# Windowed attention and a routed two-layer FFN: wider score slots, scatters without order among themselves, and q, k, v loaded in other pieces

## The chip, the cores and the metric

The kernel runs on one core of one Trainium2 chip. The metric is the device time of one execution in microseconds (us). A core has a matrix engine (PE, whose weight loads are listed apart as PEld), a vector engine (DVE), an activation engine (ACT), a general engine (POOL) and a sync engine (SP) that only issues transfers; 16 DMA engines move data between HBM and the on-chip memory. PE writes to PSUM, the accumulators; everything else lies in SBUF.

## The reference

```python
def _attn_ref(q, k, v):                       # (8, 8, 576, 64) each: batch, head, position, width
    scores = np.matmul(q, k.transpose(0, 1, 3, 2)) / np.sqrt(64)
    scores = np.where(np.abs(pos[:, None] - pos[None, :]) <= 32, scores, -1e9)
    return softmax(scores) @ v

def _moe_ref(x, modality_id, w_gate, modality_bias, w1, w2):   # x: (4608, 512), 8 experts
    logits = x @ w_gate + modality_bias[modality_id]
    e_idx = np.argmax(logits, axis=1)                          # one expert for a token
    gate_w = softmax(logits)[np.arange(N), e_idx]
    for e in range(8):                                         # w1[e]: 512x1024, w2[e]: 1024x512
        out[e_idx == e] = gate_w * (np.maximum(x @ w1[e], 0) @ w2[e])
```

## The kernel before

The work has two stages. The attention stage loops over 8 batches. The FFN stage loops over tiles of 256 tokens that have the same expert. They meet in a scratch array `scr` in HBM, where each expert has a region of rows.

Loads of a batch. q and k come in two groups of four heads, 96 partitions with six consecutive positions each (L227, runs of 1.5 KB). q is cast to bf16 on POOL (L233), k on ACT (L235). v comes in five blocks of 128 positions (L241, runs of 256 B) and is cast on POOL (L242). All of these loads are issued on SP's queue, as are the token ids (L155) and the zeros that are written to the first 256 rows of each expert's region (L199).

A batch has four pairs of heads. For each, PE transposes q and k in six pieces of 96 positions (L254); DVE copies q's transposes out of PSUM (L259), ACT copies k's (L261); one PSUM buffer `tp` serves both and the routing. Scores are computed transposed, key blocks j against the 192 queries that each can see (96 for the last block, L272). They lie side by side in slots of 192, blocks 0, 1 and 4 in one PSUM tile, 2 and 3 in another. ACT takes the exponent of each tile (L275, 960 and 768 columns), DVE multiplies by the mask (L277). The output block m then takes two products with `pt` as the weights: the 128 first columns of slot m (L288), and for m > 0 the 64 last columns of slot m - 1 (L295):

```python
nc.tensor.matmul(o_t[:, m - m0, h, :], pt[:, h, c0:c0 + P], vt[:, m, 2 * hp + h, :], ...)
if m > 0:
    nc.tensor.matmul(o_t[0:64, m - m0, h, :], pt[:, h, c1:c1 + 64], vt[:, m - 1, 2 * hp + h, :], ...)
```

DVE divides by the sum of the row, which an added column of ones in v delivers (L300, L301).

Routing of a batch. For each of five blocks PE transposes the attention output (L311), DVE copies it (L313), and PE multiplies by the gate (L315). Some 17 small DVE instructions find the expert, the gate weight and the token's row in the expert's region (`di`, L361). Five indirect DMAs issued by POOL scatter the rows of 1,088 bytes (output, gate weight, token number) into `scr` (L364). After batch 0 the weights of two experts are loaded from POOL's queue (L178, L181). After batch 7 DVE builds a table of tiles (L390 to L453).

FFN, tile i: SP loads 256 rows of `scr` (L463), PE transposes them (L467), multiplies by w1 (L490), ACT applies the relu (L492), PE multiplies by w2 (L504), DVE scales by the gate weight (L507), and POOL scatters 128 rows twice to the output by an indirect DMA (L509), with indices that DVE makes (L499). 19 tiles always run; six more stand behind a condition.

The order of instructions on each engine and all waits are made by the framework: it schedules at build time, earlier program text first, and derives a wait from each pair of accesses to the same memory. Two scatters into `scr`, or two into the output, count as such a pair, because their rows are known only at run time. Engines execute their own instructions in order.

Of the kernel before, what the change touches and what calls it, by code (L numbers as in the profile page):

```python
# [21 lines left out]
FP32 = mybir.dt.float32  # L22
# [9 lines left out]
def kernel(  # L32
# [14 lines left out]
    P = 128  # L47
# [7 lines left out]
    R = 6  # L55
    SP_ = S // R
# [21 lines left out]
    PW = 896  # L78
    SLOT = {0: 0, 1: 192, 4: 384, 2: 512, 3: 704}
    mask = const.tile([P, PW], BF16)  # L80
    nc.gpsimd.memset(mask[:], 1.0)
    for j in (0, 1, 2, 3):
        m_ap = mask[:, SLOT[j]:SLOT[j] + 192]
        nc.gpsimd.affine_select(out=m_ap, in_=m_ap, compare_op=ALU.is_ge, fill=0.0,
                                base=0, pattern=[[1, 192]], channel_multiplier=-1)
        nc.gpsimd.affine_select(out=m_ap, in_=m_ap, compare_op=ALU.is_ge, fill=0.0,
                                base=64, pattern=[[-1, 192]], channel_multiplier=1)
    m_ap = mask[:, SLOT[4]:SLOT[4] + 96]
# [25 lines left out]
    ids_i, ids_f = iota_f([P, B, NM], [[S, B], [P, NM]], -32, 1)  # L114
# [29 lines left out]
    nc.sync.dma_start(mb_bc[:], moe_modality_bias.partition_broadcast(P))  # L144

    mid = const.tile([P, B, NM], FP32)
    mid64 = const.tile([P, B, NM], mybir.dt.int64)
    nc.gpsimd.memset(mid64[:].bitcast(I32), 0)
    idv = moe_modality_id.rearrange("(b s) -> s b", s=S)
    with nc.allow_non_contiguous_dma(reason="token ids, once"):  # L150
        for m in range(NM):
            p0 = 32 if m == 0 else 0
            p1 = 96 if m == NM - 1 else P
            s0 = P * m - 32
            nc.sync.dma_start(mid64[p0:p1, :, m:m + 1], idv[s0 + p0:s0 + p1, :].unsqueeze(2))  # L155
    nc.vector.tensor_copy(mid[:].rearrange("p b m -> p (b m)").unsqueeze(2),
                          mid64[:].rearrange("p b m -> p (b m)").bitcast(I32)
                          .rearrange("p (n two) -> p n two", two=2)[:, :, 0:1])
    bias = const.tile([P, B * NM, E], FP32)
    msel = const.tile([P, B * NM], FP32)  # L160
    mtmp = const.tile([P, B * NM, E], FP32)
    for m_ in range(n_mod):
        nc.vector.tensor_scalar(out=msel[:], in0=mid[:].rearrange("p b m -> p (b m)"),
                                scalar1=float(m_), scalar2=None, op0=ALU.is_equal)
        dst = bias if m_ == 0 else mtmp
        nc.vector.tensor_tensor(
            out=dst[:], in0=msel[:].unsqueeze(2).to_broadcast([P, B * NM, E]),
            in1=mb_bc[:, m_, :].unsqueeze(1).to_broadcast([P, B * NM, E]), op=ALU.mult)
        if m_:
            nc.vector.tensor_tensor(out=bias[:], in0=bias[:], in1=mtmp[:], op=ALU.add)  # L170
# [18 lines left out]
    qT_t = [const.tile([P, 32 + S], BF16, name=f"qT{i}") for i in range(2)]  # L189
# [3 lines left out]
    for t_ in x_t:  # L193
        nc.gpsimd.memset(t_[:, :, HD // 2 + 2:ROW // 2], 0)

    zero = const.tile([P, TT // P, ROW // 2], I32)
    nc.gpsimd.memset(zero[:], 0)
    for e in range(E):
        nc.sync.dma_start(scr[N * e:N * e + TT, :].rearrange("(s p) c -> p s c", p=P), zero[:])  # L199
    for t_ in qT_t:  # L200
        nc.gpsimd.memset(t_[:, 0:32], 0.0)
    for t_ in p_t:
        nc.gpsimd.memset(t_[:, :, SLOT[4] + 96:SLOT[4] + 128], 1.0)
    for t_ in v_t:
        nc.gpsimd.memset(t_[:, :, :, D:D + 1], 1.0)
# [5 lines left out]
    with (  # L211
        tc.tile_pool(name="ld", bufs=3) as ld,
        tc.tile_pool(name="ldb", bufs=4) as ldb,
        tc.tile_pool(name="kt", bufs=2) as ktp,
# [3 lines left out]
        tc.tile_pool(name="ps_t", bufs=1, space=bass.MemoryType.PSUM) as ps_t,  # L218
        tc.tile_pool(name="ps_m", bufs=1, space=bass.MemoryType.PSUM) as ps_m,
    ):  # L220
        for b in range(B):

            qb, kb = [None, None], [None, None]
            for g in range(2):
                for nm, src, dst in (("q", q, qb), ("k", k, kb)):
                    f_ = ld.tile([SP_, 4, R * D], FP32, tag="qkf")
                    nc.sync.dma_start(  # L227
                        f_[:], src[b, 4 * g:4 * g + 4].rearrange("h (p r) d -> p h (r d)", r=R))
                    c_ = ldb.tile([SP_, R, 4 * D], BF16, tag=nm + "b")
                    o_ap = c_[:].rearrange("p r (h d) -> p h r d", h=4)  # L230
                    i_ap = f_[:].rearrange("p h (r d) -> p h r d", r=R)
                    if nm == "q":
# [3 lines left out]
                    dst[g] = c_  # L236
            vt = v_t[b % 2]
            for j in range(NM):
                s0 = min(P * j, S - P)
                f_ = ld.tile([P, H, D], FP32, tag="vf")  # L240
                nc.sync.dma_start(f_[:], v[b, :, s0:s0 + P, :].rearrange("h s d -> s h d"))  # L241
                nc.gpsimd.tensor_copy(vt[:, j, :, 0:D], f_[:])  # L242
# [3 lines left out]
            for hp in range(H // 2):  # L246
                g, l = hp // 2, 2 * (hp % 2)
                it = b * 4 + hp
                qT = qT_t[it % 2]
                kT = ktp.tile([P, S], BF16, tag="kT")  # L250
                for src, dst, eng in ((qb[g], qT[:, 32:32 + S], "v"), (kb[g], kT[:], "a")):
                    tp = ps_t.tile([P, S], BF16, tag="tp")
                    for i in range(R):
                        nc.tensor.transpose(tp[:, SP_ * i:SP_ * (i + 1)],  # L254
                                            src[:, i, D * l:D * l + P], ident[0:SP_, 0:SP_])
                    o_ap = dst.rearrange("d (p r) -> d p r", r=R)
                    i_ap = tp[:].rearrange("d (r p) -> d p r", p=SP_)
                    if eng == "v":
                        nc.vector.tensor_copy(o_ap, i_ap)  # L259
                    else:  # L260
                        nc.scalar.copy(o_ap, i_ap)  # L261
# [3 lines left out]
                for js, s_t, o0, wd in (((0, 1, 4), sA, 0, 480), ((2, 3), sB, 512, 384)):  # L265
                    for j in js:
                        c0 = SLOT[j] - o0
                        k0 = P * j if j < 4 else S - P
                        q0 = P * j
                        w_ = 192 if j < 4 else 96  # L270
# [4 lines left out]
                    nc.scalar.activation(pt[:, :, o0:o0 + wd], s_t[:, :, 0:wd], ACT.Exp, scale=scale)  # L275
                    w2_ = 512 if o0 == 0 else 384
                    nc.vector.tensor_tensor(  # L277
                        out=pt[:, :, o0:o0 + w2_], in0=pt[:, :, o0:o0 + w2_],
                        in1=mask[:, o0:o0 + w2_].unsqueeze(1).to_broadcast([P, 2, w2_]), op=ALU.mult)
# [3 lines left out]
                for o_t, m0, ms in ((oA, 0, (0, 1, 2)), (oB, 3, (3, 4))):  # L283
                    first = True
                    for m in ms:
                        for h in range(2):
                            c0 = SLOT[m]
                            nc.tensor.matmul(  # L288
                                o_t[:, m - m0, h, :], pt[:, h, c0:c0 + P], vt[:, m, 2 * hp + h, :],
                                start=first, stop=(m == 0),  # L290
                                skip_group_check=True)
                            first = False
# [14 lines left out]
            lg = ps_m.tile([P, NM, E], FP32, tag="m")  # L307
# [10 lines left out]
            nc.vector.tensor_tensor(out=lo[:], in0=lg[:], in1=bias[:, NM * b:NM * b + NM, :], op=ALU.add)  # L318
# [24 lines left out]
            rk = ps_m.tile([P, NM + 1, E], FP32, tag="m")  # L343
# [112 lines left out]
    def ffn(tiles, pools):  # L456
# [38 lines left out]
        def down(i):  # L495
# [33 lines left out]
    with (  # L529
# [45 lines left out]
```

## Time and profile before

| | |
|---|---|
| time, median of 3 runs | 503.09 us (500.39 to 504.54) |
| the profiled execution | 506.83 us |
| its span, first to last instruction | 505.1 us |
| PE busy | 344.3 us (68%) |
| DVE, ACT, POOL busy | 200.5, 144.2, 140.9 us |
| attention stage, to the last `di` | 0 to 308.7 us |
| FFN stage, to the last scatter's issue | 322.5 to 493.8 us |

Times of day below are us from the span's start. A busy share is an average over both stages, which have different limits.

### The profile page before, as it was taken

To read this page: it belongs to the slowest core of one execution; us is meant where nothing else is said; L and a number is where in the kernel's file an instruction comes from. 1 tells how busy PE (TensorE), PEld (TensorE's weight loads), DVE (VectorE), ACT (ScalarE), POOL (GpSimd) and SP (SyncE) were. 2 spreads that over 40 slices of the span, in tenths; PEclk is the share of its full clock that TensorE was granted. 3 is DMA by queue.
4 is the path that set the end of the run, shared out by engine and by line. 5 is a ranking of instruction groups with operands and counts; after the bars stand their busy time and mean duration, and the time that the engine had idled before them with its cause. 6 is when DMAs were issued, how large, how long until landed. Compare 5 with 4: busy or idle time off the path is not lost. (4 is left out here: it accounts for less than half of the span.)

```text
span 505.1 us, 7239 instructions
## 1 busy us (share of the span) xinstructions
PE 344.3 (68%) x2694; PEld 228.9 (45%) x2712; DVE 200.5 (40%) x529; ACT 144.2 (29%) x197; POOL 140.9 (28%) x225
## 2 busy tenths in 40 slices
PE   0477642675687587686785871299999987878900
PEld 0244431453454354454554540176766655546500
DVE  2434723654555654654645547122232131311400
ACT  2333432154135242341432310033323322313200
POOL 9122326334063332332300302102321222212320
PEclk9999999999999999999999999999999999999965
DMA  9999699955936785621000100302323223232120
GB/s 181 238 236 205 128 218 250 207 129 141 228 87 151 167 189 135 117 54 42 32 21 0 51 0 21 119 1 88 108 86 108 84 75 99 84 108 86 64 84 21
DMA packets 75238, 56.09 MB, mean 111 GB/s; under 512 B 49472, under 2 KB 70720, under 8 KB 75200
## 3 DMA queue, kind: packets, MB, share of 16 engines
q1 hardware_dynamic: 66576, 36.93, 33.6%
q0 software_dynamic: 8624, 18.66, 12.9%
q8 instruction: 23, 0.38, 0.3%
q14 instruction: 15, 0.12, 0.1%
HBM read 122.79 MB, written 17.76 MB: 278 GB/s over the span
## 5 line engine op out<-in xcount | busy, mean ns | idle before, releaser
L364 POOL DMA_INDIRECT scr<-xt,di x40 | 41.3, 1033 | 150.4 <-DMA scr<-xt,di 69.0
L492 ACT ACTIVATE hT<-ph 128x512 bf16<-128x512 f32 x76 | 45.4, 597 | 122.3 <-PE ph L490 122.3
L490 PE MATMUL ph<-xT,w 128*128 128x256 bf16 x608 | 70.6, 275 | 0.0
L509 POOL DMA_INDIRECT out_dram<-ys,ix x38 | 36.9, 970 | 115.6 <-DMA out_dram<-ys,ix 56.6
L504 PE MATMUL py<-w,hT 128*128 128x512 bf16 x286 | 67.6, 379 | 0.9
L490 PEld LDWEIGHTS <-w 128*128 128x128 bf16 x608 | 59.4, 99 | 7.2
L275 ACT ACTIVATE pt<-sA 128x960 bf16<-128x960 f32 x32 | 31.0, 970 | 75.0 <-PE sA L272 68.8
L288 PEld LDWEIGHTS <-pt 128*128 128x128 bf16 x320 | 29.3, 108 | 40.9 <-DVE pt L277 23.0
L295 PEld LDWEIGHTS <-pt 128*64 128x64 bf16 x256 | 32.7, 128 | 30.6 <-issue 12.9
L277 DVE TENSOR_TENSOR pt<-pt,mask 128x1024 bf16<-128x1024 bf16 x64 | 44.4, 723 | 3.9 <-ACT pt L275 3.9
L288 PE MATMUL oA<-vt,pt 128*128 128x65 bf16 x192 | 33.8, 239 | 17.2 <-DVE pt L277 15.4
L499 DVE TENSOR_TENSOR ix<-xg,pen_i 128x2 int32<-128x2 int32 x19 | 3.1, 161 | 105.7 <-DMA out_dram<-ys,ix 93.5
L504 PEld LDWEIGHTS <-hT 128*128 128x128 bf16 x304 | 29.8, 98 | 32.0
L288 PE MATMUL oB<-vt,pt 128*128 128x65 bf16 x128 | 30.1, 235 | 13.4 <-POOL vt L242 12.6
L507 DVE TENSOR_SCALAR ys<-py,xg 128x512 f32<-128x512 f32 x38 | 27.5, 748 | 17.0 <-PE py L504 15.4
L295 PE MATMUL oB<-vt,pt 128*64 128x65 bf16 x128 | 33.7, 263 | 0.0
L295 PE MATMUL oA<-vt,pt 128*64 128x65 bf16 x128 | 33.7, 263 | 0.0
L467 PE MATMUL tp<-ident,xg 128*128 128x128 bf16 x152 | 12.5, 229 | 29.1 <-DMA xg<-scr 29.1
L259 DVE COPY qT<-tp 128x576 bf16<-128x576 bf16 x32 | 24.2, 757 | 18.8 <-PE tp L254 17.5
L313 DVE COPY xT<-tp 128x512 bf16<-128x512 bf16 x40 | 16.9, 423 | 25.9 <-PE tp L311 25.9
L261 ACT COPY kT<-tp 128x576 bf16<-128x576 bf16 x32 | 20.4, 638 | 22.1 <-PE tp L254 21.8
L315 PE MATMUL lg<-wg_sb,xT 128*128 128x8 bf16 x160 | 10.7, 173 | 23.4 <-DVE xT L313 23.4
(254 smaller groups left out, 417.1 us busy)
## 6 DMA issues: line engine op xcount, KB each, us to landing
w<-in_moe_w_dram POOLq DMA_DIRECT2D x42, 1024.0 KB, 8.0
xg<-scr SPq DMA_DIRECT2D x19, 272.0 KB, 3.2
scr<-zero SPq DMA_DIRECT2D x8, 272.0 KB, 3.4
scr<-xt,di POOLq DMA_INDIRECT x40, 2.5
out_dram<-ys,ix POOLq DMA_INDIRECT x38, 2.9
f__209<-in_q_dram SPq DMA_DIRECT2D x1, 576.0 KB
f__213<-in_k_dram SPq DMA_DIRECT2D x1, 576.0 KB
f__217<-in_q_dram SPq DMA_DIRECT2D x1, 576.0 KB
```

The lines of the kernel that those rows point to most:

```text
L259: nc.vector.tensor_copy(o_ap, i_ap)
L261: nc.scalar.copy(o_ap, i_ap)
L275: nc.scalar.activation(pt[:, :, o0:o0 + wd], s_t[:, :, 0:wd], ACT.Exp, scale=scale)
L277: nc.vector.tensor_tensor(out=pt[:, :, o0:o0 + w2_], in0=pt[:, :, o0:o0 + w2_], in1=mask[:, o0:o0 + w2_].unsqueeze(1).to_broadcast([P, 2, ...
L288: nc.tensor.matmul(o_t[:, m - m0, h, :], pt[:, h, c0:c0 + P], vt[:, m, 2 * hp + h, :], start=first, stop=(m == 0), skip_group_check=True)
L295: nc.tensor.matmul(o_t[0:64, m - m0, h, :], pt[:, h, c1:c1 + 64], vt[:, m - 1, 2 * hp + h, :], start=False, stop=True, skip_group_check=True)
L364: nc.gpsimd.indirect_dma_start(out=scr[:], out_offset=bass.IndirectOffsetOnAxis(ap=di[:, m:m + 1], axis=0), in_=xi[:, m, :], in_offset=Non ...
L490: nc.tensor.matmul(ph[:, u, :], w1[:, kd, P * mi:P * mi + P], xTs[i][:, kd, :], start=(kd == 0), stop=(kd == n_kd - 1))
L492: nc.scalar.activation(hT[:, 2 * mp:2 * mp + 2, :], ph[:], ACT.Relu)
L504: nc.tensor.matmul(py[:], hTs[i][:, kf, P * s:P * s + P], w2[:, kf, :], start=(kf == 0), stop=(kf == n_kf - 1))
L507: nc.vector.tensor_scalar(out=ys[:], in0=py[:], scalar1=xg[:, s, HD // 2:HD // 2 + 1].bitcast(FP32), scalar2=None, op0=ALU.mult)
L509: nc.gpsimd.indirect_dma_start(out=out, out_offset=bass.IndirectOffsetOnAxis(ap=ix[:, s:s + 1], axis=0), in_=ys[:], in_offset=None, bounds ...
```

## The change

- **Slots.** Each of the score blocks 0 to 3 gets a slot of 256 columns in `pt`: 192 scores and 64 columns that stay zero. The second product of a block reads 128 columns (64 of scores, 64 of zeros) and writes all 128 output rows. Blocks 0 and 1 share a PSUM tile, and 2, 3 and 4 the other. Exponent and mask work on 2 x 192 columns at a time, with an instruction of 96 columns each for block 4.
- **Scatters.** Those into `scr` are declared to have no dependency on each other, and so are those into the output. The waits on the zeros, and of the FFN loads on the scatters, are written out by hand.
- **q and k.** The first 512 positions come on 128 partitions with four consecutive positions each (runs of 1 KB); the last 64 positions of all heads come apart (`rf`, runs of 256 B on 64 partitions). Transposes are four of 128 positions; the tail has eight small ones in a batch and one copy. The transposed q and k of a whole batch have a buffer, two in all.
- **v, ids, bias.** They are issued on ACT's queue; v has buffers of its own (four), and its last block is 64 positions. The ids are loaded as rows and transposed by PE. The zeros are issued in batch 0 behind its loads.
- **PSUM.** `tp` has two buffers. The gate's sums and the ranks share the buffers of `oB` and `oA`.

```diff
-    R = 6
-    SP_ = S // R
+    R = 4
+    SM = P * R
+    SR = S - SM
...
-    PW = 896
-    SLOT = {0: 0, 1: 192, 4: 384, 2: 512, 3: 704}
+    WIN, WL = 192, 96
+    SW = 256
+    PW = 4 * SW + P
...
+    def after(ins, others):
+        for o_ in others:
+            tc.add_manual_dep(ins.ins, o_.ins.name, mybir.DependencyInfo(
+                mybir.DependencyClass.Sync, mybir.DependencyReason.DATA), reason="scratch rows")
+
+    def unordered(ins, group):
+        tc.declare_no_dep(ins.ins, group=group, reason="disjoint rows")
+        tc.add_to_no_dep_group(group, ins.ins)
...
+            rf = ldr.tile([SR, 2, H, D], FP32, tag="rf")
+            nc.sync.dma_start(rf[:, 0], q[b, :, SM:S, :].rearrange("h s d -> s h d"))
+            nc.sync.dma_start(rf[:, 1], k[b, :, SM:S, :].rearrange("h s d -> s h d"))
...
-                        f_[:], src[b, 4 * g:4 * g + 4].rearrange("h (p r) d -> p h (r d)", r=R))
+                        f_[:], src[b, 4 * g:4 * g + 4, 0:SM, :].rearrange("h (p r) d -> p h (r d)", r=R))
...
-                nc.sync.dma_start(f_[:], v[b, :, s0:s0 + P, :].rearrange("h s d -> s h d"))
+                nc.scalar.dma_start(f_[p0:P], v[b, :, s0 + p0:s0 + P, :].rearrange("h s d -> s h d"))
...
+            tpr = ps_t.tile([P, H // 2, 2, SR], BF16, tag="tp")
+            for hp in range(H // 2):
+                for u in range(2):
+                    nc.tensor.transpose(tpr[:, hp, u, :], rb[:, u, P * hp:P * hp + P], ident[0:SR, 0:SR])
+            nc.vector.tensor_copy(qkT[:, :, :, 32 + SM:32 + S], tpr[:])
...
-                for js, s_t, o0, wd in (((0, 1, 4), sA, 0, 480), ((2, 3), sB, 512, 384)):
+                for j0, s_t in ((0, sA), (2, sB)):
...
-                                c1 = SLOT[m - 1] + P
+                                c1 = SW * (m - 1) + P
                                 nc.tensor.matmul(
-                                    o_t[0:64, m - m0, h, :], pt[:, h, c1:c1 + 64],
+                                    o_t[:, m - m0, h, :], pt[:, h, c1:c1 + P],
...
-                nc.gpsimd.indirect_dma_start(
+                ins = nc.gpsimd.indirect_dma_start(
                     out=scr[:], out_offset=bass.IndirectOffsetOnAxis(ap=di[:, m:m + 1], axis=0),
                     in_=xi[:, m, :], in_offset=None, bounds_check=E * N - 1, oob_is_err=False)
+                unordered(ins, "scr")
+                after(ins, zero_ins)
+                scr_ins.append(ins)
...
-            nc.sync.dma_start(xg[:], scr[bass.ds(r_r, TT), :].rearrange("(s p) c -> p s c", p=P))
+            ins = nc.sync.dma_start(xg[:], scr[bass.ds(r_r, TT), :].rearrange("(s p) c -> p s c", p=P))
+            if first_block:
+                after(ins, scr_ins)
...
-                nc.gpsimd.indirect_dma_start(
+                ins = nc.gpsimd.indirect_dma_start(
                     out=out, out_offset=bass.IndirectOffsetOnAxis(ap=ix[:, s:s + 1], axis=0),
                     in_=ys[:], in_offset=None, bounds_check=N - 1, oob_is_err=False)
+                unordered(ins, "out")
```

## Rows read from the trace of the kernel before

**Rows 1.** Busy time by stretch; columns: length, five engines, clock, DMA share, GB/s.

```profile
11.40:103.20 91.80, 52.09 (x437) 33.71 (x438) 41.81 (x115) 28.26 (x34) 28.98 (x31) 1.00 1.04 209
...
173.00:243.20 70.20, 50.69 (x418) 32.96 (x415) 38.89 (x101) 24.52 (x31) 23.26 (x24) 1.00 0.44 99
243.20:308.70 65.50, 48.52 (x390) 31.37 (x389) 33.98 (x98) 17.99 (x25) 9.90 (x10) 1.00 0.06 20
308.70:322.50 13.80, 0.00 (x0) 0.00 (x0) 5.69 (x32) 0.00 (x0) 4.97 (x9) 1.00 0.13 45
322.50:494.00 171.50, 143.16 (x1046) 98.29 (x1064) 40.98 (x76) 45.37 (x76) 37.70 (x72) 0.97 0.27 86
```

**Rows 2.** Timeline of one pair of heads; columns: start, us, instruction, idle before.

```profile
251.41 0.35 PE L288 MATMUL oA<-vt,pt 128*128 128x65 bf16 x3
...
251.69 0.26 PE L295 MATMUL oA<-vt,pt 128*64 128x65 bf16 x1
...
252.06 0.26 PE L295 MATMUL oA<-vt,pt 128*64 128x65 bf16 x1
...
254.68 0.50 PE L272 MATMUL sA<-qT,kT 64*128 64x192 bf16 x4
...
256.89 1.15 DVE L277 TENSOR_TENSOR pt<-pt,mask 128x1024 bf16<-128x1024 bf16 x2
257.02 0.64 PE L254 MATMUL tp<-ident,c__2464 96*128 96x96 bf16 x6 [0.85 <-DVE qT L259]
...
257.63 0.34 PE L288 MATMUL oA<-vt,pt 128*128 128x65 bf16 x3
```

**Rows 3.** Groups by line and shape, whole span: busy us, mean ns, idle before.

```profile
L295 PEld LDWEIGHTS <-pt 128*64 128x64 bf16 x256 | 32.7, 128 | 30.6 <-issue 12.9
L275 ACT ACTIVATE pt<-sA 128x960 bf16<-128x960 f32 x32 | 31.0, 970 | 75.0 <-PE sA L272 68.8 <-PE oB L288 3.8 <-PE oB L295 2.4
...
L288 PEld LDWEIGHTS <-pt 128*128 128x128 bf16 x320 | 29.3, 108 | 40.9 <-DVE pt L277 23.0 <-issue 3.5 <-DVE xt L301 1.4
...
L275 ACT ACTIVATE pt<-sB 128x768 bf16<-128x768 f32 x32 | 25.8, 805 | 0.0
...
L259 DVE COPY qT<-tp 128x576 bf16<-128x576 bf16 x32 | 24.2, 757 | 18.8 <-PE tp L254 17.5 <-PE sB L272 0.7
```

**Rows 4.** Timeline of PE in the routing of a batch.

```profile
268.64 0.27 PE L315 MATMUL lg<-wg_sb,xT 128*128 128x8 bf16 x4 [0.52 <-DVE xT L313]
268.77 0.59 PE L311 MATMUL tp<-ident,xt 128*128 128x128 bf16 x4
```

**Rows 5.** Timeline of PE in the FFN, the transposes that open a tile.

```profile
332.07 0.61 PE L467 MATMUL tp<-ident,xg 128*128 128x128 bf16 x8
...
391.21 0.61 PE L467 MATMUL tp<-ident,xg 128*128 128x128 bf16 x8
...
463.01 0.62 PE L467 MATMUL tp<-ident,xg 128*128 128x128 bf16 x8 [1.28 <-DMA xg<-scr]
```

**Rows 6.** Timeline of DVE in the FFN.

```profile
458.26 0.16 DVE L499 TENSOR_TENSOR ix<-xg,pen_i 128x2 int32<-128x2 int32 x1 [6.78 <-DMA out_dram<-ys,ix]
```

**Rows 7.** Timeline of the end.

```profile
473.91 7.07 PE L504 MATMUL py<-w,hT 128*128 128x512 bf16 x31
...
492.83 0.97 POOL L509 DMA_INDIRECT out_dram<-ys,ix  x1 [2.54 <-DMA out_dram<-ys,ix]
```

**Rows 8.** Timeline between the stages.

```profile
309.17 0.97 POOL L364 DMA_INDIRECT scr<-xt,di  x1 [19.78 <-DVE t L395]
...
319.97 0.97 POOL L364 DMA_INDIRECT scr<-xt,di  x1 [1.32 <-DMA scr<-xt,di]
322.51 3.04 SPq L463 DMA_DIRECT2D xg<-scr  x4
```

**Rows 9.** Timeline of SP's queue, two issues of v.

```profile
35.32 4.71 SPq L241 DMA_DIRECT2D f__622<-in_v_dram  x1
...
125.81 2.74 SPq L241 DMA_DIRECT2D f__1732<-in_v_dram  x1
```

More of the change, by code (lines that the diff above doesn't have):

```diff
@@ L143 @@
     mb_bc = const.tile([P, n_mod, E], FP32)
-    nc.sync.dma_start(mb_bc[:], moe_modality_bias.partition_broadcast(P))
-    mid = const.tile([P, B, NM], FP32)
-    mid64 = const.tile([P, B, NM], mybir.dt.int64)
+    nc.scalar.dma_start(mb_bc[:], moe_modality_bias.partition_broadcast(P))
+    mid64 = const.tile([NM * B, P], mybir.dt.int64)
     nc.gpsimd.memset(mid64[:].bitcast(I32), 0)
[L149 to L170, printed above, removed]
+    idv = moe_modality_id.rearrange("(b s) -> b s", s=S)
@@ new lines @@
+    for m in range(NM):
+        p0 = 32 if m == 0 else 0
+        p1 = 96 if m == NM - 1 else P
+        s0 = P * m - 32
+        nc.scalar.dma_start(mid64[B * m:B * m + B, p0:p1], idv[:, s0 + p0:s0 + p1])
+    midr = const.tile([NM * B, P], BF16)
+    nc.vector.tensor_copy(midr[:].unsqueeze(2),
+                          mid64[:].bitcast(I32).rearrange("p (n two) -> p n two", two=2)[:, :, 0:1])
+    bias = const.tile([P, NM * B, E], FP32)
+    with (tc.tile_pool(name="setup", bufs=1) as sup,
+          tc.tile_pool(name="setup_ps", bufs=1, space=bass.MemoryType.PSUM) as sup_ps):
+        midp = sup_ps.tile([P, NM * B], BF16)
+        nc.tensor.transpose(midp[:], midr[:], ident[0:NM * B, 0:NM * B])
+        msel = sup.tile([P, NM * B], FP32)
+        mtmp = sup.tile([P, NM * B, E], FP32)
+        for m_ in range(n_mod):
+            nc.vector.tensor_scalar(out=msel[:], in0=midp[:], scalar1=float(m_), scalar2=None,
+                                    op0=ALU.is_equal)
+            dst = bias if m_ == 0 else mtmp
+            nc.vector.tensor_tensor(
+                out=dst[:], in0=msel[:].unsqueeze(2).to_broadcast([P, NM * B, E]),
+                in1=mb_bc[:, m_, :].unsqueeze(1).to_broadcast([P, NM * B, E]), op=ALU.mult)
+            if m_:
+                nc.vector.tensor_tensor(out=bias[:], in0=bias[:], in1=mtmp[:], op=ALU.add)
@@ L186, in reg @@
                               skip_runtime_bounds_check_because="the table is clamped on chip")
-    qT_t = [const.tile([P, 32 + S], BF16, name=f"qT{i}") for i in range(2)]
+    qk_t = [const.tile([P, H // 2, 2, 32 + S], BF16, name=f"qkT{i}") for i in range(2)]
     p_t = [const.tile([P, 2, PW], BF16, name=f"pt{i}") for i in range(3)]
@@ L194 @@
         nc.gpsimd.memset(t_[:, :, HD // 2 + 2:ROW // 2], 0)
+    for t_ in qk_t:
+        nc.gpsimd.memset(t_[:, :, 0, 0:32], 0.0)
+    for t_ in p_t:
+        nc.gpsimd.memset(t_[:, :, 0:4 * SW].rearrange("p h (j c) -> p h j c", c=SW)[:, :, :, WIN:SW], 0.0)
+        nc.gpsimd.memset(t_[:, :, 4 * SW + WL:PW], 1.0)
+    for t_ in v_t:
+        nc.gpsimd.memset(t_[:, :, :, D:D + 1], 1.0)
+        nc.gpsimd.memset(t_[0:P - SR, NM - 1, :, 0:D], 0.0)
     zero = const.tile([P, TT // P, ROW // 2], I32)
     nc.gpsimd.memset(zero[:], 0)
[L198 to L205, printed above, removed]
+    zero_ins, scr_ins = [], []
+    def after(ins, others):
[5 more added lines that the diff above has]
+        tc.add_to_no_dep_group(group, ins.ins)
     base = const.tile([P, E], FP32)
@@ L235 @@
                         nc.scalar.copy(o_ap, i_ap)
-                    dst[g] = c_
+                    cb[u][g] = c_
             vt = v_t[b % 2]
             for j in range(NM):
-                s0 = min(P * j, S - P)
-                f_ = ld.tile([P, H, D], FP32, tag="vf")
-                nc.sync.dma_start(f_[:], v[b, :, s0:s0 + P, :].rearrange("h s d -> s h d"))
-                nc.gpsimd.tensor_copy(vt[:, j, :, 0:D], f_[:])
+                s0 = P * j if j < NM - 1 else S - P
+                p0 = 0 if j < NM - 1 else P - SR
+                f_ = ldv.tile([P, H, D], FP32, tag="vf")
+                nc.scalar.dma_start(f_[p0:P], v[b, :, s0 + p0:s0 + P, :].rearrange("h s d -> s h d"))
+                nc.gpsimd.tensor_copy(vt[p0:P, j, :, 0:D], f_[p0:P])
+            if b == 0:
+                for e in range(E):
+                    zero_ins.append(nc.sync.dma_start(
+                        scr[N * e:N * e + TT, :].rearrange("(s p) c -> p s c", p=P), zero[:]))
+            qkT = qk_t[b % 2]
+            tpr = ps_t.tile([P, H // 2, 2, SR], BF16, tag="tp")
[3 more added lines that the diff above has]
+            nc.vector.tensor_copy(qkT[:, :, :, 32 + SM:32 + S], tpr[:])
             xi = x_t[b % 2]
@@ L248 @@
                 it = b * 4 + hp
[L249 to L252, printed above, removed]
+                qT = qkT[:, hp, 0, :]
+                kT = qkT[:, hp, 1, 32:32 + S]
+                for u in range(2):
+                    tp = ps_t.tile([P, R, P], BF16, tag="tp")
                     for i in range(R):
[L254 to L259, printed above, removed]
+                        nc.tensor.transpose(tp[:, i, :], cb[u][g][:, i, D * l:D * l + P], ident[:])
+                    o_ap = qkT[:, hp, u, 32:32 + SM].rearrange("d (p r) -> d r p", r=R)
+                    if u == 0:
+                        nc.vector.tensor_copy(o_ap, tp[:])
                     else:
-                        nc.scalar.copy(o_ap, i_ap)
+                        nc.scalar.copy(o_ap, tp[:])
                 pt = p_t[it % 3]
@@ L264 @@
                 sB = ps_s.tile([P, 2, 512], FP32, tag="sB")
[L265 to L267 removed]
+                for j0, s_t in ((0, sA), (2, sB)):
+                    for j in (j0, j0 + 1) + ((4,) if j0 else ()):
+                        c0 = WIN * (j - j0)
                         k0 = P * j if j < 4 else S - P
                         q0 = P * j
[L270 removed]
+                        w_ = WIN if j < 4 else WL
                         for h in range(2):
@@ L304 @@
                         in1=rec[:, m0:m0 + n_, :].unsqueeze(3).to_broadcast([P, n_, 2, D]), op=ALU.mult)
-            lg = ps_m.tile([P, NM, E], FP32, tag="m")
+            lg = ps_o.tile([P, NM, E], FP32, tag="oB")
             for m in range(NM):
@@ L341 @@
                                   ids_i[:, NM * b:NM * b + NM].unsqueeze(2))
-            rk = ps_m.tile([P, NM + 1, E], FP32, tag="m")
+            rk = ps_o.tile([P, NM + 1, E], FP32, tag="oA")
             nc.tensor.matmul(rk[:, 0:NM, :], tri[:], ohb[:], start=True, stop=False,
@@ L453, with ffn @@
     nc.vector.tensor_scalar(out=pen_i[:], in0=pen[:], scalar1=float(1 << 30), scalar2=None, op0=ALU.mult)
-    def ffn(tiles, pools):
+    def ffn(tiles, pools, first_block):
         xgp, hp_, yp, ps_t, ps_h, ps_y = pools
```

66 lines of the change are left out of this document (37 added, 29 removed).

## The prediction

> **What bounds the kernel now.** I read four views in this order: busy time by stretch, the timelines of one stretch of each stage, the groups by shape, and the timelines of the seams. The stretches [rows 1] show three regimes. From 11.4 to 103.2 us the DMA engines are saturated (share 1.04, 209 GB/s), and PE works for only 52 of 92 us. By 243.2 the loads have ended (share 0.06), and the last two batches of attention take 32.75 us each, with PE busy for 24.3 and DVE for 17.0: no engine is full, so a chain through several of them sets the pace. In the FFN PE is busy for 143 of 171.5 us.
>
> The chain of a pair of heads repeats after 257.63 - 251.41 = 6.22 us [rows 2]. PE spends 254.68 - 251.41 = 3.27 us on the products with v; then come scores, exponent, mask, and the next products start just behind the first mask. Within the products the narrow ones (64 columns of weights) are 0.37 us apart, with one wide product between them, whereas three wide ones in a row take 0.35 us together, though one alone takes some 0.25: they start about 0.05 apart. Narrow and wide ones in turn do not overlap.
>
> In the FFN the same transposes open each tile [rows 5]: eight tiles from 332.07 to 391.21 at 7.39 us each, without a wait, then eight up to 463.01 at 8.98, each with a wait for its rows. What is late there is the output: DVE stands for 6.78 us until a scatter has landed [rows 6], because every scatter waits for the one before it.
>
> **FFN and seams.** Without an order among the output's scatters a tile costs PE's 7.39: eight tiles save 8 x 1.59 = 12.7. POOL then needs two issues of 0.97 for a tile, which is covered. At the end PE finishes at 473.91 + 7.07 = 480.98, but the last scatter is issued at 492.83 [rows 7], behind a backlog of landings. Unordered, it goes once DVE has scaled, about 0.9 behind PE: it saves 10.9 (8.4, if one wait of 2.54 stays). Between the stages five scatters go from 309.17 to 319.97, 2.70 apart, and the first load of the FFN follows at 322.51 [rows 8]. At 0.97 apart the fifth would go 6.9 earlier; but DVE has 5.7 us of work on the table in this stretch [rows 1], and POOL has weight loads between, so I take 6.0 (5.0 to 6.9). Sum: 29.6 (26.1 to 30.5).
>
> **Products with v.** With all weights 128 wide, 18 products at 0.05 to 0.06 apart take 1.0 us instead of 3.27. Bounds: 0.9 (18 x 0.05), and no gain at all if the spacing comes from something other than the width. I take 1.2, since the products of blocks 2 to 4 now arrive before the second and third mask (two masks take 1.15 [rows 2]): a gain of 2.07 on the chain. The added 64 rows of zeros in each cost nothing that I can see, since the streamed columns stay 65.
>
> The narrow load lasts longer than the wide one, 128 against 108 ns [rows 3]. The Trainium skill (TensorE: Matmul & The Clock Gate, section on weight-path perf modes, FWL) says that a fast load is on when 128 columns of a type other than FP32 are loaded. The trace agrees in direction; by this rule alone the gain would be certain, by the rows alone "no gain" remains a bound, and it stays a rival below.
>
> **Exponent, mask, transposes.** The first exponent has 768 columns instead of 960: 0.805 against 0.970 [rows 3], 0.17 off the chain; its mask saves about 0.1. Block 4 gets an exponent of its own (192 columns; by the slope of those two rows 0.86 ns a column and a fixed 0.15: 0.31) and a mask (some 0.25): both behind the first mask, beside PE's work. The pair's chain becomes 6.22 - 2.07 - 0.27 = 3.9. With two PSUM buffers PE no longer waits 0.85 for q's copy [rows 2], but in the pairs that wait ran beside exponent and mask, so I count nothing. DVE comes near its limit: 17.0 us a batch [rows 1], plus four masks (1.0), plus the tail's copy (at most the 0.76 of a 576-column copy [rows 3], and less is likely), less 0.07 four times: 18.5. So I take 4.1 for a pair.
>
> A batch is three such pairs plus a rest, 32.75 - 18.66 = 14.1 now, with the last products and the routing. It loses 2.07 and 0.27 again, four of the five waits of 0.52 for the copy of the routing's transposes [rows 4] (2.1), and here the 0.85, which stands alone between routing and first scores; it gains about 0.5 for the eight tail transposes. That is 9.3, and a batch 3 x 4.1 + 9.3 = 21.6. Batches with loads take (70.2 - 65.5) / 2 = 2.35 more now [rows 1], so 24.0. Bounds: DVE's 18.5 below (20.9 with loads); 25 and 28 above, if DVE and ACT, both used for most of the time, hold each other up.
>
> **Loads.** Batch 2 cannot end before the data of three batches are in: 3 x 3.54 MB (q and k 2.36, v 1.18, by their shapes), 2.2 MB of zeros, 4.2 MB of weights, together 17.0 MB. At the 209 GB/s of the saturated stretch this is 81 us. Whether 128 partitions or shorter runs change the rate no row shows; I take it as it is. The first pairs start before the last block is in, so batch 2 ends at about 81 + 2 + 17 = 100. Bounds: 85, if the rate rises so that computing sets the end (11.4 + 3 x 24), and 110. Zeros and ids no longer stand ahead of the first batch's loads on SP. They are hidden in this figure.
>
> Scatters into `scr` no longer hold POOL for 2.7 us each; POOL has 9.9 to 23 us of work in 65 to 70 [rows 1], and its casts then come in time: part of the same figure.
>
> Sum of attention: 100 + 3 x 24.0 + 2 x 21.6 = 215 against 308.7: 93.5 saved.
>
> **v on ACT's queue.** Now DMA issues stand in front of exponents. On SP one issue took 2.74 and 4.71 us when the queue was full [rows 9]; on ACT exponents and k's copies wait behind such an issue, and the chain with them. ACT is busy for 12.3 us of a batch with loads [rows 1], so half its time could cover them. Bounds: nothing, and 40 x 4.71 = 188. I take 1 us a batch for six batches: 6.
>
> The Trainium skill (DMA: Bandwidth & Descriptors, section "Issuing engines are not separate DMA queues") speaks against this part: all queues run on the same 16 engines, and another issuer saves only issue time. By it the move brings no byte earlier; the sum above has no such gain either. No row of this kernel tests it.
>
> **Sum.** 506.83 - 29.6 - 93.5 + 6 = 389.7 for an execution like the profiled one (its span, 505.1, plus 1.7 around it). The median of the runs is 3.7 below this one: **386**.
>
> **Rivals.**
> Loads or ACT hold the attention stage: all its traffic, 28.3 MB of inputs and 11.4 MB of zeros, weights and scattered rows, is 190 us at 209 GB/s. With three buffers for q and k the engines will not be full all the time; at 85%, and with a last batch behind, the stage ends at 245 instead of 221: 410, and with v's issues 416. For it: DMA share 1.04 early, so the margin is thin once computing shrinks. Against: 0.44 later.
> The products do not close up: 32 x 2.07 = 66 comes back: 452. Against it: the three wide ones in a row.
> The declaration changes nothing, because another wait orders the scatters (a semaphore shared, a buffer): 386 + 29.6 = 416.
> PE's clock rises in attention. The view prints 1.00 for all of it [rows 1], yet four transposes of 128 columns take 0.59 in the routing [rows 4] and eight take 0.61 in the FFN [rows 4, 5], so attention runs at the lower of the two levels, 1.2 GHz. If denser products raise it, those and the scores halve: about 0.8 a pair, 25 in all: 361. The Trainium skill (the same TensorE page, Part 1) has the clock follow how busy PE has been; rows 1 show PE busy for 74% of the time without a rise.
> Slower than before: every issue of v stalls ACT with an exponent behind it. From (503 - 386 + 6) / 40 = 3.1 us for each beyond what is covered, the whole gain is gone; at the 4.71 of rows 9 the time is 568. Against it: the stall came at the third of a run of issues, not at each.
>
> **How the numbers follow.** Forecast 0.62; loads or ACT 0.14; clock 0.10; products 0.06; declaration 0.05; slower 0.03. Low end: batches at DVE's floor, batch 2 at 85, is 85 + 62.7 + 37 = 185, 30 us less than the sum: with the 6 of ACT gone, 350; little of the chance lies there, so 352. High end: batch 2 at 110 and batches of 28 and 25 give 244, and 29 more than the sum is 415; with the output's order kept too it is above 440. I take 432. Only the products and the slower case lie outside whole. About 1% is what a measurement of this kernel can tell from no change: faster 0.95, within 1% 0.02, slower 0.03.
>
> **What would show it.** Right: products of 128 columns about 0.055 apart and a pair near 4.1; no wait of POOL for a scatter; FFN tiles at 7.39 to the end; the last scatter within 2 us of PE's end; the last batch done near 221. Wrong: ACT idle behind its own issues, pairs still above 5 us, DMA share near 1 beyond 150 us, or FFN tiles at 9.

## The result and the profile after

The changed kernel takes 417.78 us (median of 4, 417.38 to 418.31) beside 503.81 for the kernel before: ratio 0.830, 95% interval 0.826 to 0.835. Some executions of a kernel come out over 1.5% slower than its fastest; the ratios and the times of the kernel before, here and below, leave those out. The forecast was 386, in a range of 352 to 432. In what follows, the end of a batch is the start of the instruction that writes its index table (`di`); the profiled span is 416.7 us.

Stretches of the changed kernel (columns as in [rows 1]): batch 0 from just before its first exponent (32.98) on, batch 2, the last batch, the FFN.

```profile
31.00:57.70 26.70, 18.52 (x220) 13.08 (x219) 20.76 (x58) 18.86 (x25) 9.33 (x11) 0.76 1.00 276
...
82.70:124.20 41.50, 17.09 (x194) 12.05 (x194) 19.28 (x55) 11.81 (x17) 14.01 (x17) 0.50 0.84 179
...
228.60:248.90 20.30, 13.01 (x152) 8.97 (x149) 14.93 (x50) 8.04 (x12) 4.89 (x5) 0.50 0.09 32
...
257.10:402.60 145.50, 142.18 (x1064) 98.67 (x1064) 41.88 (x75) 45.38 (x76) 36.50 (x73) 0.98 0.29 99
```

In the FFN PE is now busy for 142 of 145.5 us (143 of 171.5 before). Batch 2 takes 41.5 us though no engine works for more than 19.3 of them.

Timelines of the changed kernel: two products with v, and the scores of the second tile in the second and third pair of the last batch; the scatters between the stages; the transposes of two FFN tiles; the end.

```profile
229.61 0.58 PE L309 MATMUL sB<-qkT 64*128 64x192 bf16 x5
...
233.70 0.24 PE L330 MATMUL oB<-vt,pt 128*128 128x65 bf16 x1
...
233.76 0.25 PE L335 MATMUL oB<-vt,pt 128*128 128x65 bf16 x1
...
234.26 0.58 PE L309 MATMUL sB<-qkT 64*128 64x192 bf16 x6
...
249.26 0.97 POOL L404 DMA_INDIRECT scr<-xt,di  x1 [14.23 <-DVE t L438]
...
250.54 0.97 POOL L404 DMA_INDIRECT scr<-xt,di  x1 [0.30 <-issue]
...
303.32 0.61 PE L512 MATMUL tp<-ident,xg 128*128 128x128 bf16 x8
...
310.71 0.61 PE L512 MATMUL tp<-ident,xg 128*128 128x128 bf16 x8
...
395.54 7.07 PE L549 MATMUL py<-w,hT 128*128 128x512 bf16 x32
...
403.67 0.97 POOL L554 DMA_INDIRECT out_dram<-ys,ix  x1 [0.76 <-DVE ys L552]
```

The products are 0.06 us apart (0.37 for two in [rows 2]); a pair repeats after 234.26 - 229.61 = 4.65 us (6.22; by the first tile's scores, two repeats take 4.81 and 4.67). The scatters of a batch are 1.28 apart (2.70 in [rows 8]), the tiles 7.39 to the end (8.98 in the second half, [rows 5]). The last scatter goes 403.67 - 402.61 = 1.06 us behind PE's end (11.85 in [rows 7]).

Groups of the changed kernel by shape: the two copies of the transposes (the first answers to 0.757 us in [rows 3]).

```profile
L296 DVE COPY qkT<-tp 128x512 bf16<-128x512 bf16 x32 | 41.4, 1295 | 20.1 <-PE tp L293 19.2
L298 ACT COPY qkT<-tp 128x512 bf16<-128x512 bf16 x32 | 41.3, 1317 | 48.6 <-PE tp L293 20.5 <-POOL rb L249 20.0 <-issue 7.9
```

There are fewer columns than before (512, not 576), and DVE's copy takes 1.7 times as long. Timelines of the changed kernel: the first load of q, and batches 1 and 2.

```profile
17.67 0.49 DVE L177 TENSOR_TENSOR bias<-bias,mtmp 128x320 f32<-128x320 f32 x1
18.19 0.39 SPq L253 DMA_DIRECT2D f__219<-in_q_dram  x1
...
68.95 8.33 ACTq L268 DMA_DIRECT2D f__1389<-in_v_dram  x1
77.33 1.29 ACT L298 COPY qkT<-tp 128x512 bf16<-128x512 bf16 x1 [7.89 <-issue]
88.02 7.93 ACTq L268 DMA_DIRECT2D f__1395<-in_v_dram  x1
91.78 0.62 POOL L269 CAST vt<-f__1386 128x512 bf16<-128x512 f32 x1 [10.21 <-DMA f__1386<-in_v_dram]
99.79 0.62 POOL L269 CAST vt<-f__1389 128x512 bf16<-128x512 f32 x1 [7.39 <-DMA f__1389<-in_v_dram]
100.58 1.06 POOL L404 DMA_INDIRECT scr<-xt,di  x1 [0.18 <-issue]
108.28 0.58 DVE L380 COPY xt<-ioi 128x5 int32<-128x5 int32 x1 [17.68 <-DMA scr<-xt,di]
```

Read in order of time: the first q load goes just when the bias table is done (five of the eight writes of zeros go ahead of it, from 12.73 us on). In batch 2, v's rows for batch 3 come late. POOL waits for them with two casts that stand ahead of batch 1's scatters, whose indices were ready at 82.60; DVE has the copy of a later batch's token numbers in its order, which waits 17.68 us for these scatters, with batch 2's masks behind it.

### The profile page after: what moved, and what is told of

It reads as the page before. It is cut to its first block, busy times and chain, and to the rows that moved or that the text cites. A ratio compares the mean times of both kernels' runs of the same rounds, so it can differ in the third digit from the quotient of the medians.

```text
span 416.7 us, 7245 instructions
## 1 busy us (share of the span) xinstructions
PE 280.7 (67%) x2649; PEld 197.0 (47%) x2649; DVE 212.2 (51%) x569; ACT 157.8 (38%) x229; POOL 141.1 (34%) x235
## 5 line engine op out<-in xcount | busy, mean ns | idle before, releaser
L298 ACT COPY qkT<-tp 128x512 bf16<-128x512 bf16 x32 | 41.3, 1317 | 48.6 <-PE tp L293 20.5
L330 PEld LDWEIGHTS <-pt 128*128 128x128 bf16 x320 | 28.9, 123 | 49.7 <-DVE pt L315 31.1
L296 DVE COPY qkT<-tp 128x512 bf16<-128x512 bf16 x32 | 41.4, 1295 | 20.1 <-PE tp L293 19.2
L330 PE MATMUL oA<-vt,pt 128*128 128x65 bf16 x192 | 25.2, 238 | 33.8 <-DVE pt L315 21.8
L315 DVE TENSOR_TENSOR pt<-pt,mask 128x768 bf16<-128x768 bf16 x64 | 37.9, 607 | 2.1 <-ACT pt L313 2.0
L313 ACT ACTIVATE pt<-sB 128x768 bf16<-128x768 f32 x32 | 25.9, 810 | 32.9 <-PE sB L309 29.2
L313 ACT ACTIVATE pt<-sA 128x768 bf16<-128x768 f32 x32 | 26.3, 821 | 13.9 <-PE sA L309 9.1
L351 PE MATMUL tp<-ident,xt 128*128 128x128 bf16 x160 | 26.6, 299 | 5.7 <-DVE xt L341 3.3
L335 PEld LDWEIGHTS <-pt 128*128 128x128 bf16 x256 | 28.5, 129 | 0.0
L309 PEld LDWEIGHTS <-qkT 64*128 64x128 bf16 x320 | 16.7, 118 | 19.1 <-ACT qkT L298 8.0
L309 PE MATMUL sA<-qkT 64*128 64x192 bf16 x128 | 16.8, 340 | 10.6 <-ACT pt L313 5.2
L309 PE MATMUL sB<-qkT 64*128 64x192 bf16 (+1 forms) x192 | 22.6, 323 | 0.1
```

The lines of the kernel that those rows point to most:

```text
L296: nc.vector.tensor_copy(o_ap, tp[:])
L298: nc.scalar.copy(o_ap, tp[:])
L309: nc.tensor.matmul(s_t[:, h, c0:c0 + w_], kT[D * h:D * h + D, k0:k0 + P], qT[D * h:D * h + D, q0:q0 + w_], start=True, stop=True)
L313: nc.scalar.activation(p_ap, s_t[:, :, 0:2 * WIN].rearrange("p h (j c) -> p h j c", c=WIN), ACT.Exp, scale=scale)
L315: nc.vector.tensor_tensor(out=p_ap, in0=p_ap, in1=mask[:].unsqueeze(1).to_broadcast([P, 2, 2, WIN]), op=ALU.mult)
L330: nc.tensor.matmul(o_t[:, m - m0, h, :], pt[:, h, SW * m:SW * m + P], vt[:, m, 2 * hp + h, :], start=(m == m0 and h == 0), stop=(m == 0), ...
```

## The experiments

All but e7 are the changed kernel with the edits named. Batches 3 to 7 are the time between the ends of batch 2 and 7. The kernel before took 503 to 509 us beside them, so a difference of 3 or 4 us between two rows proves little; the last column repeats better (124.8 and 124.9 for the same kernel).

| run | us | ratio to before, 95% interval | end of batch 2 | batches 3 to 7 |
|---|---|---|---|---|
| changed | 417.78 | 0.830 (0.826 to 0.835) | 124.1 | 124.8 |
| e8, the same again | 416.11 | 0.827 (0.817 to 0.836) | 120.7 | 124.9 |
| e1 | 413.85 | 0.814 (0.809 to 0.820) | 122.5 | 122.1 |
| e2 | 411.89 | 0.810 (0.805 to 0.815) | 121.7 | 119.6 |
| e3 | 404.78 | 0.797 (0.792 to 0.803) | 119.8 | 115.6 |
| e4 | 450.12 | 0.887 (0.881 to 0.892) | 134.9 | 145.4 |
| e5 | 413.73 | 0.821 (0.813 to 0.829) | 124.8 | 119.8 |
| e6 | 436.57 | 0.865 (0.857 to 0.873) | 130.4 | 135.3 |
| e7 | 478.10 | 0.947 (0.938 to 0.956) | 136.8 | 170.8 |
| e9 | 406.18 | 0.807 (0.802 to 0.812) | 110.2 | 126.0 |
| e10 | 409.65 | 0.813 (0.809 to 0.818) | 106.8 | 132.8 |
| e11 | 397.14 | 0.789 (0.784 to 0.794) | 100.4 | 125.9 |
| e12 | 422.24 | 0.830 (0.827 to 0.833) | 125.0 | 126.9 |

**e7, the declaration alone**, in the kernel before.

```diff
+                unordered(ins, "scr"); after(ins, zero_ins)
...
+                unordered(ins, "out")
```

> The kernel before with only the declaration: scatters into the scratch rows and into the output unordered, with the hand-written waits for zeros and for the first block's loads. Theory (the terms of the prediction): FFN tiles at 7.39 us throughout, last scatter within 2 us of PE's end, scatters between the stages 1.3 apart: 29.6 us less, and some 0 to 10 in attention, where POOL stood 69 us for scatters: 464 to 478 beside a kernel before of 504 to 508. Rival (the output's scatters only looked late; PE's 8.98 comes from the loads of rows): 490 to 505.

Two tiles, and the end:

```profile
437.42 0.61 PE L484 MATMUL tp<-ident,xg 128*128 128x128 bf16 x8
444.81 0.61 PE L484 MATMUL tp<-ident,xg 128*128 128x128 bf16 x8
455.70 7.07 PE L521 MATMUL py<-w,hT 128*128 128x512 bf16 x31
463.84 0.97 POOL L526 DMA_INDIRECT out_dram<-ys,ix  x1 [0.76 <-DVEq L561]
```

It takes 27.0 us less than the kernel before beside it (505.12), with attention ending at 307.6 as before (308.7); from there to the end the trace has 27.2 us less. The theory holds: the tiles stay at 7.39, and the last scatter goes 1.07 us behind PE's end.

**e3, copies in address order.**

```diff
-                    o_ap = qkT[:, hp, u, 32:32 + SM].rearrange("d (p r) -> d r p", r=R)
+                    o_ap = qkT[:, hp, u, 32:32 + SM].rearrange("d (p r) -> d p r", r=R)
+                    i_ap = tp[:].rearrange("d r p -> d p r")
```

> The copies of q's and k's transposes to SBUF write in address order and read PSUM with the stride, as in the kernel before; the changed kernel reads in order and writes with steps of 8 bytes. Theory (the strided write is what takes 1.295 us on DVE and 1.317 on ACT, and both copies lie on the chain of a pair of heads): the copies fall to at most 0.76 and 0.64 and the attention stage gains 0.5 to 1.2 us a pair, 16 to 38 in all: 380 to 402. Rival 1 (the copies are long for the stride, whichever side has it): durations stay at 1.2 to 1.3 us, time 416 to 419. Rival 2 (they shorten but run beside exponent and mask of the pair before): durations fall, time 412 to 418.

Groups of e3, the same two copies; then its pairs in the last batch.

```profile
L297 DVE COPY qkT<-tp 128x512 bf16<-128x512 bf16 x32 | 22.0, 689 | 19.3 <-PE tp L293 18.4
...
L299 ACT COPY qkT<-tp 128x512 bf16<-128x512 bf16 x32 | 18.6, 587 | 47.2 <-PE tp L293 27.2 <-POOL rb L249 6.8 <-DMA f__2508<-in_v_dram 6.8
```

```profile
217.57 0.58 PE L310 MATMUL sB<-qkT 64*128 64x192 bf16 x5
...
221.52 0.58 PE L310 MATMUL sB<-qkT 64*128 64x192 bf16 x6
```

Both halve, a pair takes 3.95 us, and the time falls by 13.0: short of the theory's 16, but on its side. Of this, 9.2 us are in batches 3 to 7. The strided write was the price, and it lay on the path.

**e4 and e6, the narrow second product again**, without and with e3's copies.

```diff
-                                    o_t[:, m - m0, h, :], pt[:, h, c1:c1 + P],
+                                    o_t[0:64, m - m0, h, :], pt[:, h, c1:c1 + 64],
```

> The second product with v has 64 columns of weights again, all else as in the changed kernel. Theory (alternating widths do not overlap; that is a gain of 2.07 us a pair on the chain): products 0.17 to 0.2 us apart instead of 0.055, the 32 pairs 1.5 to 2.1 us longer, time 466 to 484. Rival (DVE with 77% busy, ACT and the loads set the pace now, so PE's longer products are half covered): products as far apart, time 430 to 450. Second rival (the width does not matter; the slots' places did it): products stay at 0.055, time 417 to 419.

> Narrow second products as in e4 and copies in address order as in e3, so that the products can be priced with DVE and ACT less full. Theory (the wide products gain 2.07 us a pair on the chain, and only 1.0 of it shows in e4 because the long copies on DVE and ACT cover the rest): against e3's 404.8 the narrow products cost 1.5 to 2.07 us a pair, 48 to 66 us: 453 to 471; that is, e4's 450 does not fall. Rival (1.0 us a pair is what they are worth, whatever the copies do, since part of the products ran beside exponents): 404.8 + 32 = 437, 434 to 441.

In e4's last batch a wide and a narrow product in turn take 0.36 us, much as in [rows 2] (0.37):

```profile
261.00 0.26 PE L335 MATMUL oA<-vt,pt 128*64 128x65 bf16 x1
...
261.36 0.26 PE L335 MATMUL oA<-vt,pt 128*64 128x65 bf16 x1
```

The width alone costs 32.3 us (e4) and 31.8 (e6), 1.0 a pair, whatever the copies do. That is e6's rival; e4's time lies at the edge of its rival's range, but the long copies do not cover the rest, as e6 shows. In the last batch, which runs alone, a pair of e6 takes 5.72 us, 1.77 more than e3's (e4 against the changed kernel: 6.43 and 4.65), close to the forecast's 2.07:

```profile
243.22 0.58 PE L310 MATMUL sB<-qkT 64*128 64x192 bf16 x5
...
248.94 0.58 PE L310 MATMUL sB<-qkT 64*128 64x192 bf16 x6
```

e6's last batch is 6.5 us longer than e3's, batches 4 to 6 only 3.3 to 3.6: where two batches run into each other, about half of the products' added time is covered. By what, no run tells.

**e1, e2, e5, e12: one suspect of batch 2 at a time.** e1: `msel` and `mtmp` from the pool of constants. e2: `nc.sync` for v's loads. e5: the weight loads written behind the scatters of batches 2 to 5. e12: three row buffers.

```diff
+                e_rs = [reg(sp_i[0:1, i:i + 1], [ET.Pool], 0, E - 1) for i in range(2)]
+            if 2 <= b <= 5:
+                load_w(1 + b % 2, (b - 2) // 2, e_rs[(b - 2) // 2])
```

> The two temporaries of the bias table keep memory of their own, instead of memory that the q/k load buffers take over later. Theory (the first q/k loads, at 18.19 us, wait for the bias table to be finished at 18.16, because they write into its memory): the first q/k load is issued before 5 us, the first exponent comes near 20 instead of 32.98, and since batch 0 and batch 1 are then 11 to 13 us earlier the whole is 405 to 408. Rival (the DMA engines are full until batch 2 whatever the order, share 0.84 to 1.05 up to 152 us): batch 0 is earlier, but batch 2's last index table is still written near 124 us and the time is 414 to 418. Second rival (the wait is for something else than the memory): first q/k load still at 18, time 417 to 418.

The first load goes at 2.38 us and the first exponent at 26.6; batch 2 gains 1.6. The mechanism is the theory's, the gain nearly the rival's: here PE waits in batch 2, for v's casts.

```profile
104.00 0.21 PE L330 MATMUL oB<-vt,pt 128*128 128x65 bf16 x1 [8.81 <-POOL vt L269]
```

> v's loads are issued by SP behind q's and k's, as in the kernel before, all else as in the changed kernel. Theory (three v issues of 8.33, 4.29 and 7.93 us in batch 2 stand ahead of exponents on ACT and hold the chain): ACT has no DMA issue and no idle time behind one, batch 2 ends near 105 to 110 instead of 124, and the time is 400 to 405. Rival (the issues are long only because the DMA engines are full; the wait moves to SP and the data come no earlier): batch 2 ends at 120 to 126 and the time is 414 to 420.

It takes 5.9 us less, mostly behind batch 2, whose end moves by 2.4. The time fits neither; the rival is right on batch 2, in which the DMA share is 1.02.

> The four 1 MB weight loads are issued one by one behind the scatters of batches 2 to 5, instead of all behind those of batch 0; the choice of experts is still made after batch 0. Theory (4.2 MB of weights ahead of batch 2's and 3's rows of v hold POOL's casts, those hold the scatters of batch 1 in POOL's order, and DVE waits 17.68 us for these scatters): no wait of DVE for a scatter above 5 us, no issue of v above 4 us, batch 2 takes 25 to 29 us instead of 41.5, and the time is 402 to 407. Rival (the bytes have to be moved in any case and will push later batches, each by some 5 us): batch 2 shorter, batches 3 to 6 longer by as much in all, time 414 to 420.

This run tests neither, because the edit hardly moved the loads: the framework placed three of the four in batch 1 again (the changed kernel issues its four from 64.46 to 66.93 us), and the fourth at 96.75. The time, 413.7, is no evidence on the weights, and why batches 3 to 7 take 5.0 us less is not known. In batch 1 ACT stands behind two issues of v (10.19 and 7.79 us), and the first begins among the weight loads:

```profile
69.06 0.80 POOL L186 DMA_DIRECT2D w<-in_moe_w_dram  x1 [0.64 <-DVE pt L321]
70.88 0.94 POOL L189 DMA_DIRECT2D w<-in_moe_w_dram  x1
71.17 10.19 ACTq L268 DMA_DIRECT2D f__1389<-in_v_dram  x1
72.43 0.76 POOL L186 DMA_DIRECT2D w<-in_moe_w_dram  x1
...
89.31 1.29 ACT L298 COPY qkT<-tp 128x512 bf16<-128x512 bf16 x1 [18.32 <-issue]
```

Whether the weights make v's issues long is therefore open.

> The changed kernel with three buffers instead of two for the rows that are scattered. Theory (the copy of the token ids for batch 3 is placed early on DVE, in the middle of batch 2, and there waits 17.68 us for the scatters of batch 1, and 2.4 to 2.9 us in each batch behind it; with a third buffer it waits for scatters that landed a batch ago): no wait of DVE for a scatter, batch 2 done at 106 to 112 instead of 121 to 124, later batches 1 to 3 us shorter, time 393 to 405. Rival (v's casts, late behind the weights, hold PE in batch 2 until the same moment): DVE's wait is gone, PE waits for rows of v in its place, batch 2 at 118 to 124, time 412 to 418.

Both miss, since the wait did not go:

```profile
109.18 0.58 DVE L380 COPY xt<-ioi 128x5 int32<-128x5 int32 x1 [16.27 <-DMA scr<-xt,di]
```

Three of these copies now stand at 5.6 us and one at 66.9, so by count this is batch 4's: the framework used the new buffer to place the copy a batch earlier, and it waits for the same scatters. What this wait alone costs is not measured.

**e9, e10, e11: together.** e9 is the edits of e2 and e5; e10 adds e1's; e11 adds e3's. Here too the framework chose the place of the weight loads: e9 issues them at 62.70, 65.03, 82.26 and 93.29 us (e2 from 60.62 to 63.09), e10 from 54.89 to 62.07, e11 from 50.48 to 57.66, all of the last two in batch 1.

> v's loads on SP (as in e2) and the weight loads behind batches 2 to 5 (as in e5), together. Alone they gave 5.9 and 2.4 to 4.1 us of some 417. Theory (two causes cover each other: with the weights late, ACT's issue queue still fills in batch 1, 18.3 us of idle ACT; with v on SP, the weights still stand ahead of batch 2's rows; only without both can batch 2 close up): index table of batch 2 written at 103 to 108 instead of 121 to 125, time 393 to 400. Rival (the bytes themselves set batch 2's end, in any order and from any queue): batch 2 at 117 to 122, time 405 to 411, no more than the two gains added.

Batch 2 ends 11.4 us before e2's and 14.5 before e5's: together the two edits do far more than each alone, though batch 2 does not come down to the theory's 103 to 108 and the time lies in the rival's range. How much of it the two later weight loads do, and how much the order that the framework made anew, no run tells. In time only 5.7 us against e2 are left, because batches 3 to 7 take 6.4 longer; the last of them alone 1.2, with no weights to load. In these batches DVE's reciprocals (L340) stand for 17.8 us in all, 10.3 in e2, and in each batch one of them now waits for a transpose of PE (0.6 to 3.0 us), as none does in e2. So the waits, too, changed with the edit; this is a reading of the trace, not a test.

> The same two, and the bias table's temporaries in memory of their own (as in e1, which alone ended batch 2 at 122.5). Theory (the late first load is a third cause, covered in e1 by the two others): first q/k load before 5 us, batch 2 done 6 to 11 us earlier than in e9, near 96, time 384 to 392. Rival (the DMA engines are full from the start to batch 2's end, so an earlier first load moves nothing): batch 2 within 2 us of e9's, time within 3 us of e9's.

Batch 2 ends 3.4 us earlier and the batches behind it take 6.7 longer: both miss.

> All four: temporaries kept, v on SP, weights late, copies in address order. Theory (batches with loads at 23.8 us and 19.3 for the last, as in e3, behind a batch 2 that ends near 95): attention ends near 210, time 371 to 380, below the 386 forecast. Rival (with computing shorter, the loads alone set the pace of the first batches): batch 2 not earlier than in e10, only the later batches 1.9 us shorter each: 377 to 388.

Batch 2 ends at 100.4, and this is the fastest kernel here. On batch 2 the theory (near 95) is closer than the rival, but the time fits neither: the batches behind it take 25.2 us on average, with e3's 23.1 not reached. Two rows of e11, from batches 4 and 7, give one reading: PE waits for the cast of v's last block, which stands on POOL behind five scatters.

```profile
135.31 0.22 PE L331 MATMUL oB<-vt,pt 128*128 128x65 bf16 x1 [4.00 <-POOL vt L269]
...
212.82 0.21 PE L331 MATMUL oB<-vt,pt 128*128 128x65 bf16 x1 [3.57 <-POOL vt L269]
```

Such a wait stands in each of the batches 3 to 7 of e11 (20.0 us in all) and of e10 (16.5), and in none of e3's or e9's. It stands in the last batch too, when the loads are over. So it fits the longer batches better than a lack of data does; it was not tested.

**e8, the changed kernel again.**

> The changed kernel as it is, on the chip and beside the run of the kernel before that the experiments of this call have. Both theories: 415 to 420, with the same two stalls in batch 2; a difference of more than 3 us from 417.8 would be the size of what one call cannot be compared with another by.

The time is 1.7 us lower, with batch 2's end 3.4 us earlier and the batches behind it the same: that end moves by some 3 us from run to run.

## Why the prediction was right and wrong

**FFN and seams: right.** 29.6 us were forecast; from the end of attention on, the traces have 27.2 less in e7 and 28.5 less in the changed kernel (167.9 against 196.4). Tiles stand at 7.39, the last scatter goes 1.06 behind PE.

**Products with v: right mechanism, size off.** They close up to 0.055, as forecast, and the gain of 2.07 a pair is 1.77 in the last batch, but 1.0 over all 32 pairs. By the rule of the Trainium skill quoted in the prediction (TensorE: Matmul & The Clock Gate, weight-path perf modes) a load of 128 columns is a fast one and one of 64 is not; e4 agrees, with 32.3 us for the width.

**Exponent, mask, transposes: a term mis-sized.** The step that q's copy costs "less 0.07 four times" failed. It was priced from the old copy, which wrote in order and read with a stride; the new one writes with steps of 8 bytes: 1.295 us on DVE, and 1.317 on ACT for k, which had no term. In e3 the chain comes out as forecast: 3.95 a pair against 4.1, and 115.6 for batches 3 to 7 against 3 x 24.0 + 2 x 21.6 = 115.2. That the sum fits so closely is in part luck: the last batch takes 19.3 for 21.6, and batches 3 and 6 take 25.9 for 24.0 and 22.9 for 21.6. The changed kernel takes 124.8 for the five: 9.6 of the 32 us.

**Loads: the step "Batch 2 cannot end before the data of three batches are in" failed as the term that sets batch 2's end.** Batch 2 ended at 124, not 100. It does not lack its own rows: the last block of its v is cast at 67.9, and the engines moved 276 GB/s in batch 0, more than the 209 assumed. By the waits in the trace it stands for rows of batch 3, through three queues that work in order (ACT's issues, POOL's casts, DVE's early copy). No run takes this chain apart: e12's wait did not go, and e5's weight loads hardly moved. None of the edits to v's queue, the early load, the copies or the weights moves batch 2's end by more than 4.3 us, where some 3 are noise; all four together end it at 100.4. So it is shown that the edits do far more together than apart, but not which wait each of them removes, and what part the weights have stays open. That batch 2 then comes out at the forecast's 100 does not prove the forecast's sum. The assumption that zeros and ids no longer stand ahead of the first loads of q and k failed too: these wait until 18.19 us for the bias table, whose memory they take over, as e1 shows, and five writes of zeros go first.

**v on ACT's queue: right in sign and, as a sum, in size.** 6 us were forecast, and e2 gives 5.9; so close a fit is luck, since batch 2's end alone moves by 3 from run to run. The cost was put at 1 us in each batch. It comes in long issues in batch 2, of 8.33, 4.29 and 7.93 us, two of them far above the 4.71 of [rows 9], and one idle stretch of ACT behind them is 7.89 us: one of the signs of being wrong that the prediction named. The section "Issuing engines are not separate DMA queues" of the Trainium skill (DMA: Bandwidth & Descriptors) held against this part: no gain from the second queue shows here.

**The sum.** 24 us of batch 2 and 9.6 of the batches behind it, less the 6 that stood apart for ACT, are the 27.8 (by rounding 27.6) by which the attention stage missed 221 (248.8). The rest is mostly the 3.7 taken off for the median: the changed kernel's profiled execution, 418.3, is within 0.6 of its median.

**The rivals.** "Loads or ACT hold the attention stage" names 416 and the time is 418, but loads at 85% of the engines through the whole stage are not what happened: the DMA share is 0.84 in batch 2 and 0.43 to 0.61 in batches 3 to 5. Its part for ACT, 6 us, is the one that the forecast has too. The clock did not rise (last section), the products closed up, the declaration worked, and ACT's stalls stayed far from 3.1 us at each issue.

## What to carry to other kernels

A copy is priced by which side carries the stride, so a term may be taken from an old row only if its access pattern is the same. Where engines work in order, ask of each load which instruction waits for it and what of an earlier batch stands behind that one; a batch can be held up by the rows of the next. Single fixes of such a coupling show almost nothing, so try them together before one is dismissed. Where a framework makes the order of instructions, look in the trace at where the edited instruction went: e5 moved the text of the weight loads by two batches and more, and three of the four loads by some 5 us; e9 to e11 got other waits in batches that they were not meant to touch.

## What the runs showed of the hardware

The printed clock does not tell PE's speed in the attention stage. In e1 it falls from 1.00 (2.4 GHz) to 0.50 (1.2 GHz) half-way; the 20 transposes of a routing (PE busy is the first sum after the length) take the same, 3.46 us:

```profile
83.00:122.50 39.50, 3.46 (x20) 1.70 (x20) 1.00 0.82 176
...
172.00:198.00 26.00, 3.46 (x20) 1.75 (x20) 0.50 0.51 138
```

In both stretches four of them in a row take 0.59 us, while eight in the FFN take 0.61 [rows 4, 5], so by their length PE runs at the lower level in both. That such transposes do follow the clock is seen in the changed kernel's FFN, where the first tile's eight take 1.01 us and the third's 0.61:

```profile
260.05 1.01 PE L512 MATMUL tp<-ident,xg 128*128 128x128 bf16 x8 [12.17 <-DMA xg<-scr]
...
266.36 0.61 PE L512 MATMUL tp<-ident,xg 128*128 128x128 bf16 x8
```

The four executions of e11 print a mean clock of 0.985, 0.881, 0.72 and 0.724, and their times agree within 0.7%.

A write of 2-byte elements with steps of 8 bytes takes 1.9 times as long on DVE (1295 against 689 ns) and 2.2 times on ACT (1317 against 587) as the same copy with the stride on the PSUM side. The Trainium skill (SBUF — State Buffer, Door 1: The DMA port swizzle) says that two accesses to each line of 16 bytes are enough for full bandwidth; by it these writes would be free. The measurement decides.
